# A linear attention with a gated feed-forward on one core: the gates of four chunks by seven block products in place of eight, with the order of the work searched anew

## The chip, the cores and the metric

The kernel runs on one core of one Trainium2 chip. The core has a matrix engine (TensorE, PE in the profile, with its weight loads shown apart as PEld), a vector engine (VectorE, DVE), a scalar engine (ScalarE, ACT), a general engine (GpSimd, POOL) and SyncE (SP), which here only starts transfers. Each engine works through its own queue of instructions in the order in which they stand there; waits between engines go by semaphores. Sums of matrix products are made in eight banks of PSUM, each 128 partitions of 512 f32 numbers. Data and results lie in HBM and are moved to and from the on-chip memory SBUF by DMA.

The metric is the time of one execution on the device in microseconds (us), of which a lower one is better.

## The reference

Inputs are q, k and v of 8 batches, 8 heads, 576 rows and 64 columns, and four weight matrices: w1 and w2 (512 x 1024), w3 (1024 x 1024) and w_out (1024 x 512).

```python
def phi(x):
    return np.where(x > 0, x, np.exp(x) - 1.0) + 1.0
q_p, k_p = (phi(q), phi(k))
kv = np.einsum('bhsd,bhse->bhde', k_p, v)
z = np.sum(k_p, axis=2)
num = np.einsum('bhsd,bhde->bhse', q_p, kv)
den = np.einsum('bhsd,bhd->bhs', q_p, z)[..., None] + 1e-06
x = (num / den)  # heads side by side: 4608 tokens x 512
a = x @ w1
b = x @ w2
h = a * b @ w3
out = h @ w_out
```

## The kernel before

Tokens are in 36 tiles of 128 (two sets of 64 rows of one batch each); four tiles make a chunk of 512 tokens, of which there are nine, 0 to 8. All matmuls are bf16, all sums f32.

The weights come first: w3 and w_out are multiplied into one matrix wf = w3 @ w_out (steps T3, FW), which is kept in bf16, so that the feed-forward is two products by w1 and w2 (the gates a and b), their elementwise product, and one product by wf.

The whole program is a list of steps, the string `ORDER`. A step is written `KIND.arguments`, with a last letter for the engine where there is a choice (`a` ACT, `v` DVE, `p` POOL, `s` SP). The steps are emitted in the order of the string, so the string sets the order of each engine's queue; nothing moves them later. The steps that matter:

- `LQ`, `LK`, `LV` (b, h): load of q, k or v of batch b and half h of the heads, 576 KB each, on SP's queue.
- `PT`, `EX`, `PM` (q or k, b, h): phi, as max(x,0)+1 on DVE, exp(x) on ACT and the minimum of both on DVE.
- `VC` (b, h): cast of v to bf16. `KB` (b): the products of k by v on PE, then a copy.
- `QD` (b, h): transpose of phi(q) by DMA on SP's queue. `ND` (t): numerator and denominator of tile t. `NT` (t): those of the three tiles t to t+2, a "trio", 48 small matmuls into two tiles of PSUM, then 1/denominator (tile `r`) on DVE; `NM` (t, i): the four multiplies with r on DVE that make the tokens `xn` of the trio.
- `XD` (c, m): transpose of two token tiles of chunk c to `xt` by DMA on SP's queue.
- `F` (c, f): for chunk c and block f of 128 gate columns: four matmuls 128x512 for a, four for b, a copy of a to SBUF on ACT, and a multiply with b on DVE, which makes `ab`.
- `O` (t): eight matmuls of the `ab` of tile t by wf, and a copy to `o_sb` by ACT or DVE. `S` (t): its store, two pieces of 128 KB, on SP's queue. `Q` (35): the last tile in narrower pieces with its own stores.

PSUM is split: four banks named "mm", which a, b and the O tiles take, and two tiles "at" of two banks each, which the trios and the attention take. A tile of a bank is free again when what reads it is done. Buffers of SBUF rotate: four for the exp, four for each phi, five for `o_sb`, thirteen of 128x1152 f32 for raw loads ("ld").

In the profile the a and b matmuls are line 483, the ACT copy of a 492, the DVE multiply 494, the O matmuls 536 and their copies 543, the numerators 399, r 431 to 433, their multiplies 405, the phi of PT 286 and PM 294, the cast of v 328, exp 274, and the loads 158.

Of the kernel before, what the change touches and what calls it, by code (L numbers as in the profile page):

```python
# [58 lines left out]
S.26.s S.27.s F.7.7 F.8.0 F.8.1 F.8.2 O.28.v O.29.v S.28.s O.30.a O.31.v F.8.3 S.29.s S.30.s S.31.s
F.8.4 F.8.5 F.8.6 F.8.7 O.32.v O.33.v S.32.s O.34.a S.33.s S.34.b Q.35  # L60
"""


@with_exitstack
def kernel(
    ctx: ExitStack,
    tc: tile.TileContext,
    q: bass.AP,
    k: bass.AP,
    v: bass.AP,  # L70
    moe_w1: bass.AP,
# [532 lines left out]
```

## Time and profile before

| What | Value |
| --- | --- |
| Median of the device time, 3 runs | 241.37 us (241.37 to 241.63) |
| Profiled execution: span, and the median of the runs less the span | 239.7 us, 1.7 us |
| Instructions in it | 5540 |
| PE busy | 233.2 us, 97% of the span |
| DVE busy | 151.0 us, 63% |
| ACT busy | 115.0 us, 48% |
| POOL busy | 8.1 us, 3% |
| Read from HBM, written to it | 38.80 MB, 9.44 MB |

Busy time is the union of the times in which an engine had an instruction at work. The span runs from the first to the last instruction of the profiled execution; the profile has no other time of that execution, and the median of the runs is 1.7 us longer than its span. Groups are shown as line, engine, operation, output<-inputs with partitions x elements and type, the count after an x, then busy us and mean ns of one, then the engine's idle time ahead of them and what ended most of it. The mean of one matmul (380 ns for 128x512) holds its pipelined end, so that four of them in a row take less than four times as long.

### The profile page before, as it was taken

The page shows a single profiled execution, that of the slowest core. Times are in us where ns is not written, and L with a number is a line of the kernel's source. Part 1 is how long each engine was busy: PE and PEld are TensorE (multiplying, and loading weights), DVE is VectorE, ACT ScalarE, POOL GpSimd, SP SyncE. Part 2 cuts the span into 40 slices and gives each one's busy share as a digit, 9 for nine tenths or more (in the row PEclk, how much of TensorE's full clock was granted, in tenths as well). Part 3 has the DMA queues.
Part 4 walks back from the last instruction along what each step waited for, and adds up shares of the span by engine and source line. Part 5 has one row for each costly group of instructions (what it writes and reads, how often), then busy time and mean ns, then how long its engine had stood idle before and what let it go on. Part 6 is the DMA issues. An engine that isn't in the chain of part 4 may idle for free.

```text
span 239.7 us, 5540 instructions
## 1 busy us (share of the span) xinstructions
PE 233.2 (97%) x2276; PEld 120.2 (50%) x2276; DVE 151.0 (63%) x278; ACT 115.0 (48%) x173; POOL 8.1 (3%) x15
## 2 busy tenths in 40 slices
PE   8899999999999999999999999999999999999994
PEld 5656668555445444444454444545444444444443
DVE  0347787889999646877862588885546363433341
ACT  2576743979793255568522656424232113321300
POOL 1020053000000000000000000000000000000000
PEclk9999999999999999999999999999999999999999
DMA  6999999999996999999879959965293763005216
GB/s 241 402 406 397 379 375 390 390 390 389 396 332 137 158 357 247 323 406 296 190 106 192 392 123 262 320 116 131 52 178 69 174 157 88 3 0 125 50 24 154
DMA packets 52553, 55.81 MB, mean 233 GB/s; under 512 B 31280, under 2 KB 32560, under 8 KB 52528
## 3 DMA queue, kind: packets, MB, share of 16 engines
q1 hardware_dynamic: 52288, 55.19, 78.5%
q8 instruction: 18, 0.29, 0.5%
q10 hardware_dynamic: 240, 0.26, 0.3%
q14 instruction: 7, 0.06, 0.1%
HBM read 38.80 MB, written 9.44 MB: 201 GB/s over the span
## 4 chain that ended last, share of the span: by engine, by line
PE 96%; DVE 1%; ACT 1%; issue 0%
PE o_ps L536 26%; PE a_ps L483 25%; PE b_ps L483 24%; PE wf_ps L264 6%; PE nd L399 3%; PE w3p L252 3%; PE warm L149 2%; PE kbp L341 2%; PE a_ps L516 2%; PE b_ps L516 2%; PE xp L458 1%; PE qp L369 1%; PE kvp L341 1%; ACT wo_sb L218 0%; ACT w3b L238 0%; DVE w3t L253 0%
## 5 line engine op out<-in xcount | busy, mean ns | idle before, releaser
L483 PEld LDWEIGHTS <-w_sb 128*128 128x128 bf16 x544 | 52.6, 98 | 62.5 <-DVE xt L459 0.3
L494 DVE TENSOR_TENSOR ab<-a_sb,b_ps 128x512 bf16<-128x512 f32 x68 | 46.2, 686 | 39.9 <-PE b_ps L483 38.6
L492 ACT COPY a_sb<-a_ps 128x512 f32<-128x512 f32 x68 | 39.8, 586 | 64.0 <-PE a_ps L483 63.6
L483 PE MATMUL a_ps<-xt,w_sb 128*128 128x512 bf16 x272 | 69.9, 380 | 0.0
L483 PE MATMUL b_ps<-xt,w_sb 128*128 128x512 bf16 x272 | 69.8, 379 | 0.0
L536 PE MATMUL o_ps<-wf_sb,ab 128*128 128x512 bf16 (+2 forms) x304 | 65.2, 368 | 0.0
L536 PEld LDWEIGHTS <-ab 128*128 128x128 bf16 x304 | 28.4, 98 | 31.7 <-issue 0.4
L543 ACT COPY o_sb<-o_ps 128x512 f32<-128x512 f32 x22 | 12.9, 586 | 33.5 <-PE o_ps L536 26.7
L405 DVE TENSOR_TENSOR xn<-nd,r 128x512 bf16<-128x512 f32 (+2 forms) x47 | 23.8, 559 | 0.3
L274 ACT ACTIVATE ek<-k 128x1152 bf16<-128x1152 f32 x16 | 18.7, 1172 | 0.7 <-ACT ek L274 0.7
L274 ACT ACTIVATE eq<-q 128x1152 bf16<-128x1152 f32 x16 | 18.7, 1168 | 0.4 <-DMA q<-in_q_dram 0.4
L543 DVE COPY o_sb<-o_ps 128x512 f32<-128x512 f32 x13 | 9.0, 691 | 15.3 <-PE o_ps L536 12.6
L264 PE MATMUL wf_ps<-wo_sb,w3t 128*128 128x512 bf16 x64 | 15.6, 380 | 0.5 <-ACT wo_sb L218 0.5
L286 DVE TENSOR_SCALAR phq<-q 128x1152 bf16<-128x1152 f32 x16 | 12.0, 755 | 2.7 <-DMA q<-in_q_dram 2.7
L294 DVE TENSOR_TENSOR phk<-phk,ek 128x1152 bf16<-128x1152 bf16 x16 | 11.9, 750 | 1.8 <-ACT ek L274 1.7
L294 DVE TENSOR_TENSOR phq<-phq,eq 128x1152 bf16<-128x1152 bf16 x16 | 12.1, 755 | 1.0 <-ACT eq L274 0.8
L286 DVE TENSOR_SCALAR phk<-k 128x1152 bf16<-128x1152 f32 x16 | 12.0, 753 | 0.0
L264 PEld LDWEIGHTS <-w3t 128*128 128x128 bf16 x64 | 5.9, 98 | 5.8 <-issue 0.7
L328 ACT CAST vt<-v 128x1152 bf16<-128x1152 f32 x7 | 8.1, 1162 | 0.9 <-DMA v<-in_v_dram 0.9
L253 ACT CAST w3t<-w3p 128x512 bf16<-128x512 f32 x7 | 4.0, 587 | 9.3 <-PE w3p L252 7.4
L399 PEld LDWEIGHTS <-qt 64*64 64x64 bf16 x576 | 6.1, 106 | 4.3 <-issue 4.1
L399 PE MATMUL nd<-kv,qt 64*64 64x65 bf16 x576 | 7.6, 194 | 0.4 <-DVE w3t L253 0.4
(57 smaller groups left out, 127.4 us busy)
## 6 DMA issues: line engine op xcount, KB each, us to landing
q<-in_q_dram SPq DMA_DIRECT2D x16, 576.0 KB, 8.3
k<-in_k_dram SPq DMA_DIRECT2D x16, 576.0 KB, 9.5
v<-in_v_dram SPq DMA_DIRECT2D x16, 576.0 KB, 10.5
out_dram<-o_sb SPq DMA_DIRECT2D x69, 128.0 KB, 2.5
w<-in_moe_w_dram SPq DMA_DIRECT2D x7, 512.0 KB, 10.9
wo<-in_moe_w_out_dram SPq DMA_DIRECT2D x4, 512.0 KB, 8.2
wa<-in_moe_w_dram SPq DMA_DIRECT2D x4, 512.0 KB, 10.7
wb<-in_moe_w_dram SPq DMA_DIRECT2D x4, 512.0 KB, 10.4
```

What stands on the lines that cost most here:

```text
L264: nc.tensor.matmul(wfs[i], w3ts[i][:, c, :], wo_sb[:, c, :], start=(c == 0), stop=(c == FC - 1))
L274: nc.scalar.activation(out=t, in_=raw[n, b, h], func=AF.Exp)
L286: (nc.gpsimd if e == "p" else nc.vector).tensor_scalar(out=by_set(n, t), in0=by_set("k", raw[n, b, h]), scalar1=0.0, scalar2=1.0, op0=ALU. ...
L294: nc.vector.tensor_tensor(out=t, in0=t, in1=by_set("k", es[n, b, h]), op=ALU.min)
L399: nc.tensor.matmul(dst[g * R:(g + 1) * R], qts[b, a // 2][rows, j, a % 2 * R:(a % 2 + 1) * R], kvs[b][rows, a // 2, a % 2, :], start=True, ...
L405: nc.vector.tensor_tensor(out=xn[:, :, a0:a1], in0=n4[:, :, :, 0:D], in1=r.unsqueeze(3).to_broadcast([P, 2, a1 - a0, D]), op=ALU.mult)
L483: nc.tensor.matmul(ops_[key][:, tiles.start * P:tiles.stop * P], w[:, w_row(kc), f * P:(f + 1) * P], xts[c0][:, tiles, kc, :], start=(kc = ...
L492: nc.scalar.copy(out=a_sbs[c0, f], in_=ops_[key])
L494: nc.vector.tensor_mul(out=abs_[c0][:, f, :], in0=a_sbs[c0, f], in1=ops_[key])
L516: nc.tensor.matmul(p, w[:, w_row(kc), f * P:(f + 1) * P], xts[c0][:, 2 * g:2 * g + 2, kc, :], start=(kc == 0), stop=(kc == KC - 1))
L536: nc.tensor.matmul(o_ps, abs_[c0][:, f, m * P:(m + 1) * P], wf_sb[:, f, cols], start=(f == 0), stop=(f == FC - 1))
L543: copy_of(e)(out=o_sbs[t], in_=o_ps)
```

## The change

For the pairs of chunks (5, 6) and (7, 8) the 32 steps F are replaced by the Strassen form in Winograd's version. A pair's gate for one side (a by w1 or b by w2) is a product of matrices that are each cut in 2 x 2 blocks: over the 512 inputs (two halves of 256) and the gate columns (two halves of 512) for w, and over the inputs and the two chunks for x. The four output blocks are then sums of seven products of blocks and not of eight. New steps:

- `WP` (c, f, side, i): product i of 1 to 7 for pair c, block f (0 to 3) and side 0 or 1: two matmuls 128x512 into a bank. The products 1, 5 and 6 are copied to SBUF by ACT; 2, 3 and 7 are added from the bank to such a copy by DVE; product 4 of side 0 is copied by ACT and of side 1 multiplied from the bank on DVE. For side 1, the results of 2, 3 and 7 are then multiplied with those of side 0 by POOL (f32 by f32 to bf16, 24 of them).
- `WS` (side, i): the sums of blocks of the weights, and `WT` (c, i): those of the blocks of xt, on DVE, 128x1024 bf16 each, eight of each.
- `RB`: the "at" tiles' pool is closed and their four banks are opened as single ones ("bk"), which the products take.

Eight output tiles stand in place of five: three of every eight take the space of `w3t`. `ORDER` is the same up to the step `PT.k.2.0`, about 60 us into the span, and another one behind it: all attention now stands ahead of the first WP. Of the changed string the diff shows the place of the bank change only.

```diff
+PAIRS = (5, 7)
+WIDE = ()
...
 ORDER = """
...
+NM.27.2 NT.33 S.8.s NM.33.0
+WS.1.4.v S.9.s O.12.a WS.0.4.v O.18.a XD.7.0 NM.33.1 NM.33.2 NT.30 WT.5.1.v WT.5.2.v NM.30.0 NM.30.1
+NM.30.2 XD.8.1 RB WP.5.1.0.1 WP.5.0.0.1 O.17.v WP.5.0.0.5 WP.5.1.0.5 WT.5.3.v WP.5.0.0.6 XD.8.0
...
+WP.7.3.1.4 O.31.v S.21.s O.29.v S.29.s S.31.s O.20.v O.33.v S.23.s O.34.a S.20.s S.33.s O.32.v S.34.b
+O.28.v S.32.s O.30.a S.28.s S.30.s Q.35
...
+    def ws_of(side, i):
+        if side == 0:
+            return wo_sb.rearrange("p c n -> p (c n)").rearrange("p (i r n) -> p i r n", i=4, r=2)[:, i - 1]
...
+    def s_WS(side, i, e):
+        w = (w1_sb, w2_sb)[side]
+        a, b, op = {1: (w_half(w, 0, 1), w_half(w, 1, 1), ALU.add),
+                    2: (ws_of(side, 1), w_half(w, 0, 0), ALU.subtract),
+                    3: (w_half(w, 0, 0), w_half(w, 0, 1), ALU.subtract),
+                    4: (w_half(w, 1, 0), ws_of(side, 2), ALU.subtract)}[i]
+        (nc.gpsimd if e == "p" else nc.vector).tensor_tensor(out=ws_of(side, i), in0=a, in1=b, op=op)
+
+    def s_WT(c0, i, e):
+        b11, b12, b21, b22 = x_half(c0, 0), x_half(c0 + 1, 0), x_half(c0, 1), x_half(c0 + 1, 1)
+        a, b = {1: (b12, b11), 2: (b22, xs_of(c0, 1)), 3: (b22, b12), 4: (b21, xs_of(c0, 2))}[i]
+        (nc.gpsimd if e == "p" else nc.vector).tensor_tensor(out=xs_of(c0, i), in0=a, in1=b, op=ALU.subtract)
+
+    def w_mm(ps, c0, f, side, i, first):
...
+        for r in range(2):
+            nc.tensor.matmul(ps, lhs[:, r, f * P:(f + 1) * P], rhs[:, :, r, :],
+                             start=(first and r == 0), stop=(r == 1), skip_group_check=not first)
...
+    def w_add(c0, f, side, ps, tmp, c, g, e):
+        nc.vector.tensor_tensor(out=tmp, in0=ps, in1=tmp, op=ALU.add)
+        if side == 0:
+            wtmp[c0, f, "a", c, g] = tmp
+        else:
+            (nc.gpsimd if e == "p" else nc.vector).tensor_mul(
+                out=w_ab(c0, f, c, g), in0=wtmp.pop((c0, f, "a", c, g)), in1=tmp)
+
+    def s_RB(e):
+        at_pool.close()
+        pools["bk"] = at_pool.enter_context(tc.tile_pool(name="bk", bufs=1, space=bass.MemoryType.PSUM))
+
+    def s_WP(c0, f, side, i, e):
+        q = c0, f, side
+        bank = q + ("z" if i in (3, 5) else "x" if i == 2 else "y",)
+        if i == 2:
+            wbank[bank] = mm_tile("wx" + "ab"[side], bank)
+        elif i in (1, 5):
+            wbank[bank] = take("bk", bank, [P, NCH], F32, "w" + bank[3] + "ab"[side])
+        ps = wbank[bank]
+        w_mm(ps, c0, f, side, i, i in (1, 2, 5))
+        if i in (1, 5, 6):
+            t = wtmp[q + (i,)] = w_tmp({1: "e", 5: "phq", 6: "phk"}[i], "p" + str(i) + "ab"[side])
+            nc.scalar.copy(out=t, in_=ps)
+        elif i == 2:
+            w_add(c0, f, side, ps, wtmp.pop(q + (1,)), 0, 0, e)
+            give("mm", bank)
+        elif i == 3:
+            w_add(c0, f, side, ps, wtmp.pop(q + (6,)), 1, 0, e)
+            give("bk", bank)
+        elif i == 7:
+            w_add(c0, f, side, ps, wtmp.pop(q + (5,)), 1, 1, e)
+        elif side == 0:
+            t = wtmp[c0, f, "a", 0, 1] = w_tmp("a_sb", "p4a")
+            nc.scalar.copy(out=t, in_=ps)
+        else:
+            nc.vector.tensor_mul(out=w_ab(c0, f, 0, 1), in0=wtmp.pop((c0, f, "a", 0, 1)), in1=ps)
+        if i == 4:
+            give("bk", bank)
...
```

How the instructions stand. The first place is DVE behind the last step that both orders share, `PT.k.2.0` (the first row; `vt_74` or `vt_78` is the v of an even or odd batch, `phk` and `phq` the phi of k and q). Before:

```order
L286 TENSOR_SCALAR phk<-k 128x1152
L294 TENSOR_TENSOR phk<-phk,ek 128x1152
L294 TENSOR_TENSOR phq<-phq,eq 128x2x9x64
L328 CAST vt_74<-v 128x18x64
L494 TENSOR_TENSOR ab<-a_sb,b_ps 128x512 x2
L286 TENSOR_SCALAR phk<-k 128x1152
```

With the change:

```order
L301 TENSOR_SCALAR phk<-k 128x1152
L343 CAST vt_78<-v 128x18x64
L309 TENSOR_TENSOR phq<-phq,eq 128x2x9x64 x2
L509 TENSOR_TENSOR ab<-a_sb,b_ps 128x512
L301 TENSOR_SCALAR phq<-q 128x2x9x64
L509 TENSOR_TENSOR ab<-a_sb,b_ps 128x512
```

The cast `VC.3.1` of v of batch 3 now stands directly behind the phi of k, and the first gate's multiply (F.1.1) behind that cast and two multiplies of phi of q.

On SP, at the same place, the loads before, beginning with `LV.3.0`, `LV.2.1` and `LV.3.1`:

```order
L158 DMA v<-in_v_dram 128x2x576 x3
L158 DMA q<-in_q_dram 128x2x576
L549 DMA out_dram<-o_sb 64x512 x2
L158 DMA q<-in_q_dram 128x2x576
L158 DMA v<-in_v_dram 128x2x576
```

With the change:

```order
L173 DMA v<-in_v_dram 128x2x576 x3
L173 DMA k<-in_k_dram 128x2x576
L173 DMA q<-in_q_dram 128x2x576
L173 DMA k<-in_k_dram 128x2x576 x2
L173 DMA q<-in_q_dram 128x2x576
```

A load of k of batch 5 now stands ahead of q of batch 2, and the stores of the first output tiles have moved back.

The second place is the bank change. On PE before, the end of the last trio, there NT.33, followed by an O:

```order
L399 LDWEIGHTS qt
L399 MATMUL nd<-kv,qt 64x65
L536 LDWEIGHTS ab
L536 MATMUL o_ps<-wf_sb,ab 128x512
L536 LDWEIGHTS ab
```

With the change, the end of the last trio, now NT.30 (`wya` is a bank of a product for side a):

```order
L414 LDWEIGHTS qt
L414 MATMUL nd<-kv,qt 64x65
L645 LDWEIGHTS w_sb
L645 MATMUL wya<-xt,w_sb 128x512
L645 LDWEIGHTS w_sb
```

The products `WP.5.1.0.1` and `WP.5.0.0.1` follow the trio directly, and an O (O.17) only behind them. On DVE, with the change, from the first multiply of the trio NT.33 on (`ws` and `wo_sb` are sums of weights, `xs` sums of xt):

```order
L420 TENSOR_TENSOR xn<-nd,r 128x512
L629 TENSOR_TENSOR ws<-w_sb,ws 128x1024
L629 TENSOR_TENSOR wo_sb<-w_sb,wo_sb 128x1024
L420 TENSOR_TENSOR xn<-nd,r 128x2x192
L420 TENSOR_TENSOR xn<-nd,r 128x2x64
L420 TENSOR_TENSOR xn<-nd,r 128x512
L446 TENSOR_SCALAR r<-nd 128x14
L447 TENSOR_SCALAR r<-nd 128x10
L448 RECIPROCAL r<-r 128x24
L634 TENSOR_TENSOR xs<-xt 128x1024
L634 TENSOR_TENSOR xs<-xt,xs 128x1024
L420 TENSOR_TENSOR xn<-nd,r 128x512
```

Two sums of weights stand between the multiplies of NT.33, and two sums of xt between r and the multiplies of NT.30.

More of the change, by code (lines that the diff above doesn't have):

```diff
@@ L93 @@
     ps = ctx.enter_context(tc.tile_pool(name="ps", bufs=1, space=bass.MemoryType.PSUM))
-    free = {"ld": deque(range(13)), "mm": deque(range(4)), "at": deque(range(2))}
+    at_pool = ctx.enter_context(ExitStack())
+    pools = {"mm": ps, "at": at_pool.enter_context(tc.tile_pool(name="at", bufs=1, space=bass.MemoryType.PSUM))}
+    free = {"ld": deque(range(13)), "mm": deque(range(4)), "at": deque(range(2)), "bk": deque(range(4))}
     turns = {"w3t": 3, "e": 4, "phk": 4, "phq": 4, "kv": 2, "qt": 4, "xn": 3, "xt": 4, "r": 4,
@@ L530, in s_FP, with ab_of @@
             f_out(c0, f, side)
+    def ab_of(c0, f):
+        for c in range(2):
+            if c0 - c in PAIRS and c0 - c not in WIDE:
+                return quads[c0 - c, f % 4][:, c, f // 4]
+        return abs_[c0][:, f]
     def o_mm(t, cols):
@@ L535, in o_mm @@
         for f in range(FC):
-            nc.tensor.matmul(o_ps, abs_[c0][:, f, m * P:(m + 1) * P], wf_sb[:, f, cols],
+            nc.tensor.matmul(o_ps, ab_of(c0, f)[:, m * P:(m + 1) * P], wf_sb[:, f, cols],
                              start=(f == 0), stop=(f == FC - 1))
@@ L541, in s_O @@
         o_ps = o_mm(t, slice(0, DM))
-        o_sbs[t] = take("o_sb", None, [P, DM], F32, "o_sb")
+        if t % 8 in (1, 4, 6):
+            o_sbs[t] = take("w3t", None, [P, FC, P], BF16, "o_sb").rearrange("p c t -> p (c t)").bitcast(F32)
+        else:
+            o_sbs[t] = take("o_sb", None, [P, DM], F32, "o_sb")
         copy_of(e)(out=o_sbs[t], in_=o_ps)
         give("mm", "o_ps")
+        c0 = t // CT - (t // CT - 1 in PAIRS)
+        if c0 in PAIRS and c0 not in WIDE:
+            n = uses["o", c0] = uses.get(("o", c0), 0) + 1
+            if n == 2 * CT:
+                for f in range(FC // 2):
+                    give("ld", ("abq", c0, f))
     def store(queues, t, o_sb, cols):
@@ L563, in s_Q, with late, w_half, x_half @@
             store((nc.sync, nc.scalar), t, o_sb, slice(pieces[0][0], pieces[-1][1]))
+    quads, wsum, xsum, wbank, wtmp, uses = {}, {}, {}, {}, {}, {}
+    def late(key, n):
+        t = take("ld", key, [P, HW], F32, key[0]).bitcast(BF16)[:, 0:n * NCH]
+        return t
+    def w_half(w, k, fh):
+        return w[:, 2 * k:2 * k + 2, fh * NCH:(fh + 1) * NCH]
+    def x_half(c0, k):
+        return xts[c0][:, :, k::2, :]
+    def ws_of(side, i):
+        if side == 0:
+            return wo_sb.rearrange("p c n -> p (c n)").rearrange("p (i r n) -> p i r n", i=4, r=2)[:, i - 1]
+        key = ("ws", side, (i - 1) // 2)
+        if key not in wsum:
+            wsum[key] = late(key, 4).rearrange("p (i r n) -> p i r n", i=2, r=2)
+        return wsum[key][:, (i - 1) % 2]
@@ new lines, in xs_of @@
+    def xs_of(c0, i):
+        key = ("xs", c0, (i - 1) // 2)
+        if key not in xsum:
+            xsum[key] = late(key, 4).rearrange("p (i m r n) -> p i m r n", i=2, m=CT, r=2)
+        return xsum[key][:, (i - 1) % 2]
+    def s_WS(side, i, e):
[5 more added lines that the diff above has]
+        (nc.gpsimd if e == "p" else nc.vector).tensor_tensor(out=ws_of(side, i), in0=a, in1=b, op=op)
@@ new lines, in w_tmp, with w_ab @@
+    def w_tmp(kind, name):
+        if kind == "a_sb":
+            return take(kind, None, [P, NCH], F32, name)
+        t = take(kind, None, [P, HW], BF16, name)
+        return t.bitcast(F32)[:, 0:NCH]
+    def w_ab(c0, f, c, g):
+        if c0 in WIDE:
+            if c0 + c not in abs_:
+                abs_[c0 + c] = take("ab", None, [P, FC, NCH], BF16, "ab")
+            return abs_[c0 + c][:, f + 4 * g]
+        if (c0, f) not in quads:
+            quads[c0, f] = late(("abq", c0, f), 4).rearrange("p (c g n) -> p c g n", c=2, g=2)
+        return quads[c0, f][:, c, g]
```

101 lines of the change are left out of this document (62 added, 39 removed).

## The prediction

> **What bounds the kernel now.** I read the first part of the page for the busiest engine, its chain that ended last for what the end hangs on, then the groups for durations and the stretches for how full each engine is.
>
> ```profile
> span 239.7 us, 5540 instructions
> PE 233.2 (97%) x2276; PEld 120.2 (50%) x2276; DVE 151.0 (63%) x278; ACT 115.0 (48%) x173; POOL 8.1 (3%) x15
> PE 96%; DVE 1%; ACT 1%; issue 0%
> 59.77:236.14 176.37, 176.37 (x1665) 83.66 (x1664) 111.07 (x201) 76.48 (x117) 0.00 (x0) 1.00 0.73 186
> 213.66 6.91 PE o_ps L536 x32
> 229.20 6.96 PE o_ps L536 x48
> ```
>
> PE is 96% of the chain. The fourth row is the stretch 59.77:236.14 (PE, PEld, DVE, ACT, POOL busy, granted clock, DMA share, GB/s): PE is never idle there, at clock 1.00. The fifth row, of the chain in order of time, prices a 128x512 matmul: 6.91 / 32 = 0.216 us. The last row ends at 236.16; what follows, 239.7 − 236.16 = 3.5 us, is copy and stores. So the end moves with PE: a matmul removed is worth 0.216 us, and a PE wait added costs its whole length. The profiled execution's span is 239.7, the median 241.37; the 1.7 us outside the span I add unchanged.
>
> **The part removed.** A pair's gates took 16 F, each 4+4 matmuls, for two chunks: 256 matmuls for both pairs. They become 112 products of 2: 224. The 32 that go are worth 32 x 0.216 = −6.9 us. Were that all, the time would be 241.4 − 6.9 = 234.5. The rest of the sum is what the new order adds on a PE that has no slack.
>
> **The part added 1: the bank change.** The last trio, NT.30, fills both "at" tiles. The first products need these banks, and the order puts them right behind NT.30 on PE, O.17 only behind two of them. The first product's wait is on the last multiply that reads the trio's second tile, and DVE has r, two sums of xt (128x1024) and four multiplies to run in between. Such a trio before, here NT.4, had an O behind it, which needs none of this:
>
> ```profile
> 52.76 0.63 PE L399 MATMUL nd<-kv,qt 64*64 64x65 bf16 x48
> 53.33 1.90 PE L536 MATMUL o_ps<-wf_sb,ab 128*128 128x512 bf16 x8
> ...
> 53.29 0.17 DVE L431 TENSOR_SCALAR r<-nd 128x14 f32<-128x14 f32 x1
> 53.48 0.17 DVE L432 TENSOR_SCALAR r<-nd 128x10 f32<-128x10 f32 x1
> 53.69 0.30 DVE L433 RECIPROCAL r<-r 128x24 f32<-128x24 f32 x1
> 54.02 1.95 DVE L405 TENSOR_TENSOR xn<-nd,r 128x512 bf16<-128x512 f32 x4
> 55.89 0.75 DVE L286 TENSOR_SCALAR phq<-q 128x1152 bf16<-128x1152 f32 x1
> ```
>
> r takes 54.02 − 53.29 = 0.73, the multiplies 55.89 − 54.02 = 1.87. No row has a sum of two bf16 tiles 128x1024; the nearest is phk by ek, both bf16, 128x1152, quoted below, 0.68 from start to start (61.12 to 61.80): 0.68 x 1024 / 1152 = 0.60 each. With 0.15 for the handoff: 0.73 + 1.20 + 1.87 + 0.15 = 3.95, on PE from the end of NT.30, taken as **+4.0**. Bounds: a sum at half that row, 3.4; at the price of two 512-column reads of a bank (1.37, row L494 below), 5.5.
>
> **The part added 2: the trio ahead.** NT.30 itself waits for both "at" tiles from NT.33. DVE has r 0.73, multiplies 1.87, and now two sums of weights between them (1.20, priced as above), with a handoff 3.95; PE's cover is O.12 and O.18, 16 x 0.216 = 3.46. **+0.5**; bounds 0 to 2.0, by the same two prices of a sum.
>
> **The part moved: 60 to 75 us.** The two orders part at 60 us. A step of v's cast now stands on DVE directly behind the phi of k, ahead of the first gate's multiply, and its load lands late:
>
> ```profile
> 50.71 1.27 SPq L158 DMA_DIRECT2D v<-in_v_dram  x1
> ...
> v<-in_v_dram SPq DMA_DIRECT2D x1, 576.0 KB, 12.1
> 60.26 0.76 DVE L286 TENSOR_SCALAR phk<-k 128x1152 bf16<-128x1152 f32 x1
> 61.12 0.76 DVE L294 TENSOR_TENSOR phk<-phk,ek 128x1152 bf16<-128x1152 bf16 x1
> 61.80 0.75 DVE L294 TENSOR_TENSOR phq<-phq,eq 128x1152 bf16<-128x1152 bf16 x1
> 62.46 0.76 DVE L328 CAST vt<-v 128x1152 bf16<-128x1152 f32 x1
> 63.13 1.28 DVE L494 TENSOR_TENSOR ab<-a_sb,b_ps 128x512 bf16<-128x512 f32 x2
> ...
> 59.77 1.03 PE L483 MATMUL a_ps<-xt,w_sb 128*128 128x512 bf16 x4
> 60.63 1.03 PE L483 MATMUL b_ps<-xt,w_sb 128*128 128x512 bf16 x4
> 61.49 1.03 PE L483 MATMUL a_ps<-xt,w_sb 128*128 128x512 bf16 x4
> 62.36 1.03 PE L483 MATMUL b_ps<-xt,w_sb 128*128 128x512 bf16 x4
> 63.22 1.03 PE L483 MATMUL a_ps<-xt,w_sb 128*128 128x512 bf16 x4
> 64.08 1.03 PE L483 MATMUL b_ps<-xt,w_sb 128*128 128x512 bf16 x4
> ```
>
> Issued at 50.71, this v lands at 50.71 + 12.1 = 62.8; its issue lies ahead of the place where the orders part, so the time holds. DVE did two multiplies and another cast from 61.12 to 63.13; now it stands from about 60.9 to 62.8, then does the cast and two multiplies (0.67 each) and F.1.1's multiply at 62.8 + 2.0 = 64.8 to 65.45. That multiply frees the bank that F.1.0's b matmuls take, the sixth group of four, which PE could begin at 64.08 as the last row has it. They begin at 65.5: +1.4. The second wait there is a load. A k of batch 5 is put ahead of q of batch 2 on SP, whose phi and exp (DVE and ACT) stand ahead of F.1.3's multiply and F.1.0's copy:
>
> ```profile
> 54.00:62.00 8.00, 8.00 (x65) 4.13 (x64) 7.80 (x16) 7.20 (x10) 0.00 (x0) 1.00 1.05 389
> 62.56 0.59 ACT L492 COPY a_sb<-a_ps 128x512 f32<-128x512 f32 x1 [1.12 <-PE a_ps L483]
> ```
>
> At 389 GB/s with the DMA full, a 576 KB load takes 590 / 389 = 1.5 us, so that q lands not 1.5 but 3.0 us behind the v, near 65.8. ACT then does its exp and one of k before F.1.0's copy, which I place 0.8 us behind the PE that wants its bank. Together **+2.2**. Bounds: 0, if the loads land some 2 us earlier than in this row; 3.2, if the wait for q reaches PE whole (1.4 + 1.8).
>
> **Are the engines beside PE full later?** Until the first product DVE gets nearly all its phi work of batches 5 to 7 and the weight sums.
>
> ```profile
> 60.26:149.00 88.74, 88.74 (x927) 41.92 (x926) 65.53 (x119) 51.19 (x76) 0.00 (x0) 1.00 0.96 260
> L483 PE MATMUL a_ps<-xt,w_sb 128*128 128x512 bf16 x272 | 69.9, 380 | 0.0
> L494 DVE TENSOR_TENSOR ab<-a_sb,b_ps 128x512 bf16<-128x512 f32 x68 | 46.2, 686 | 39.9 <-PE b_ps L483 38.6
> L492 ACT COPY a_sb<-a_ps 128x512 f32<-128x512 f32 x68 | 39.8, 586 | 64.0 <-PE a_ps L483 63.6
> ```
>
> Before, DVE is 65.5 of 88.7 us busy there. Counting its new steps up to the first product (44 phi, 32 gate multiplies, 36 of numerators, 10 sums, casts and r) by these start-to-start prices gives about 85 of some 89 us. That leaves 4 us of slack, cover enough for the work but not for stalls; gone, each phi more would cost PE 0.67. In the products, 56 operations of 0.686 and four more sums, 41 us, and 56 copies of 0.586, 33 us, stand beside 224 x 0.216 = 48 us of products and 18 O tiles of 1.7, so no engine is full. What can cost is the order: before, a bank was read out 62.56 + 0.59 − 62.36 = 0.8 us after its successor group began; now each of the 112 products is read by a copy or an add, and PE takes the same bank again only some products later. Going through these waits one by one with the prices above, PE is late by 0.1 to 0.2 us at some six of them: **+1.0** (0.3 to 3).
>
> **POOL** gets 24 multiplies of two f32 tiles. The nearest rows:
>
> ```profile
> L222 POOL CAST w_sb<-wa 128x1024 bf16<-128x1024 f32 x3 | 3.3, 1085 | 18.9 <-DMA wa<-in_moe_w_dram 18.9
> L218 POOL CAST wo_sb<-wo 128x1024 bf16<-128x1024 f32 x1 | 1.4, 1368 | 10.1 <-DMA wo<-in_moe_w_out_dram 10.1
> ```
>
> A 512-column multiply reads as many elements as the 1024-column cast: 0.55 (half a cast) to 1.37, taken 1.1. Twenty-four take 26 of 80 us, under cover of the products; only the last five, behind which the last O stand, could show, from 1.3 each on. [...]
>
> **The end.** Q's own matmuls, copies and stores stay. Ahead of Q's stores, SP had S.33 whole and one half of S.34, whose other half went by ACT; now it has S.28 and S.30 whole:
>
> ```profile
> out_dram<-o_sb SPq DMA_DIRECT2D x69, 128.0 KB, 2.5
> ```
>
> One half more is 131 KB at 389 GB/s: **+0.3** (0 to 0.7, both of S.30).
>
> **Sum:** −6.9 + 4.0 + 0.5 + 2.2 + 1.0 + 0.3 = +1.1: span 240.8, time **242.5**. All low ends: −6.9 + 3.4 + 0.3 = −3.2 (238.2); all high ends, −6.9 + 5.5 + 2.0 + 3.2 + 3.0 + 0.7 = +7.5, would need five mishaps.
>
> **The rivals.**
>
> *A, only the bank change costs.* If the loads land so that the cast does not wait, and the waits of the products are hidden, what is left is −6.9 + 4.0 + 0.5 + 0.3 = −2.1: **239.3**, faster. For it: the deciding load's landing is one sample, and 4 us of DVE slack can take a late cast in. Against it: PE waits for F.1.1's multiply within 4 us, before slack can help. It decides if the v lands before 61.4.
>
> *B, the whole gain.* If PE had work during the bank change too: **235**. Against it: nothing stands between NT.30 and the first product.
>
> *C, the clock drops in the gap.* After its last matmul at 236.16 PE idles in the trace of before:
>
> ```profile
> 239.00:239.30 0.30, 0.00 (x0) 0.00 (x0) 0.00 (x0) 0.00 (x0) 0.00 (x0) 0.89 0.00 0
> 239.30:239.60 0.30, 0.00 (x0) 0.00 (x0) 0.00 (x0) 0.00 (x0) 0.00 (x0) 0.50 0.00 0
> ```
>
> The granted clock (third number from the right) falls to 0.50 at about 239.24, 3.1 us after the last matmul. The gap of 4.0 us is longer. If the clock takes as long to come back, 3.1 us at half speed lose 1.6: 242.5 + 1.6 = **244.1**. Against it: one drop does not say that each gap of 3.1 us makes one. [...]
>
> *D, POOL is slow.* At 1.6 us a multiply, the last five end 5 x 0.3 = 1.5 behind the O that read their outputs, and the O of the pair before wait for the sixth and seventh from the end: **244.5** or more. It decides above 1.3 us.
>
> **How the numbers follow.** The forecast 0.50, A 0.30, B 0.05, C 0.10, D 0.05. Its own range is 241.0 to 244.2 (one of its terms gone, or one at its high end). A measurement of this kernel tells 0.2% from no change, 240.9 to 241.9 counts as the same. Of the forecast's 0.50, 0.40 lies above that, 0.07 in it, 0.03 below; of A, 0.27 below and 0.03 in it. Slower: 0.40 + 0.10 + 0.05 = 0.55; same: 0.07 + 0.03 = 0.10; faster: 0.03 + 0.27 + 0.05 = 0.35. Leaving out B, D and the outer ends of A and C, some 0.15, the range is 238.0 to 245.0.
>
> **What would show it.** PE idle about 4 us behind the last trio, its releaser the DVE multiplies, and there the granted clock (C if it falls); DVE idle until about 62.8 behind a phi, released by v's load, and PE idle near 64 to 68; the groups of the products with 224 matmuls; the POOL multiply's mean (D above 1.3 us). It is wrong if PE's gap at the bank change is under 3 us, if PE has no idle time before 75 us, or if the products' stretch has over 3 us of it.

## The result

The changed kernel takes 245.29 us (245.02 to 245.51, 4 runs) against 241.37 us before: a ratio of 1.0157, 95% interval 1.0129 to 1.0185. It is slower by 3.9 us, where the prediction had 242.5 us and a range of 238.0 to 245.0: the sign is right, the size three and a half times too small. The page after:

```profile
span 243.3 us, 5583 instructions
PE 228.9 (94%) x2244; PEld 117.6 (48%) x2244; DVE 176.3 (72%) x318; ACT 126.4 (52%) x197; POOL 38.3 (16%) x39
PE 78%; DMA 8%; DVE 6%; ACT 2%; issue 2%; SPq 2%; ACTq 0%; DVEq 0%
```

PE has 32 matmuls less (2276 to 2244), and yet the span is 3.6 us longer. The third row is the chain's share by engine: 96% PE before, now 78%. The rest of the chain runs over loads and transposes, DVE, ACT and SP, because at some places PE waited for them; a share of the chain is not PE's idle time. Where PE waits stands in its order of time: start, duration, the run of matmuls, and in brackets the idle time ahead with its releaser.

```profile
63.08 1.03 PE L498 MATMUL a_ps<-xt,w_sb 128*128 128x512 bf16 x4
65.30 1.02 PE L498 MATMUL b_ps<-xt,w_sb 128*128 128x512 bf16 x4 [1.19 <-DVE ab L509]
...
68.81 1.02 PE L498 MATMUL a_ps<-xt,w_sb 128*128 128x512 bf16 x4 [0.77 <-ACT a_sb L507]
...
86.35 1.02 PE L498 MATMUL a_ps<-xt,w_sb 128*128 128x512 bf16 x4 [0.65 <-DMA xt<-xn]
...
89.90 0.58 PE L414 MATMUL nd<-kv,qt 64*64 64x65 bf16 x48
90.41 1.04 PE L498 MATMUL a_ps<-xt,w_sb 128*128 128x512 bf16 x4
...
132.72 1.02 PE L498 MATMUL a_ps<-xt,w_sb 128*128 128x512 bf16 x4 [0.84 <-ACT a_sb L507]
...
152.95 0.74 PE L414 MATMUL nd<-kv,qt 64*64 64x65 bf16 x48
157.45 1.89 PE L645 MATMUL wya<-xt,w_sb 128*128 128x512 bf16 x4 [3.75 <-DVE xn L420]
159.12 2.76 PE L557 MATMUL o_ps<-wf_sb,ab 128*128 128x512 bf16 x8
161.72 1.03 PE L645 MATMUL wza<-xs,wo_sb 128*128 128x512 bf16 x4
...
181.25 0.59 PE L645 MATMUL wyb<-xs,w_sb 128*128 128x512 bf16 x2 [0.32 <-DVE p5b L665]
...
223.64 15.74 PE L557 MATMUL o_ps<-wf_sb,abq 128*128 128x512 bf16 x88
```

The bracket starts at a matmul's modelled end, 0.16 us behind the moment at which the next could have started: 4 matmuls from 63.08 would let the next begin at 63.08 + 4 x 0.216 = 63.95, it begins at 65.30, so 1.35 us are lost where the bracket says 1.19. Behind the small matmuls of a trio it is less, 0.07: the trio from 89.90 ends at 90.48, and the gate's matmul behind it, which waits for nothing, starts at 90.41. The waits at 86, 132 and 157 us stand behind a trio. With 0.16 or 0.07 added, the losses are 1.35, 0.93, 0.72, 0.91, 3.82 and 0.48 us.

One loss has no bracket. The 12 matmuls from 157.45 to 161.72 take 4.27 us, at 0.216 they would take 2.59: 1.68 us more. The stretches there (the last three columns are granted clock, DMA share, GB/s):

```profile
157.40:157.60 0.20, 0.15 (x1) 0.13 (x2) 0.00 (x0) 0.00 (x0) 0.00 (x0) 0.63 1.25 267
...
160.60:160.80 0.20, 0.20 (x2) 0.00 (x0) 0.00 (x0) 0.00 (x0) 0.00 (x0) 0.50 1.02 297
160.80:161.00 0.20, 0.20 (x2) 0.12 (x1) 0.00 (x0) 0.00 (x0) 0.00 (x0) 0.84 0.85 184
```

The granted clock falls to one half within the first row and comes back in the last. A mean of 0.63 over 0.20 us is 1.00 for a quarter of it and 0.50 for the rest, so it falls at 157.45; in the same way it comes back at 160.86.

The sum: −6.9 (matmuls) + 2.28 (the two losses at 64 and 68 us) + 0.72 + 0.91 (at 86 and 132 us) + 0.16 (the last trio takes 0.74 where others take 0.58) + 3.82 (the gap at the bank change) + 1.68 (half clock) + 0.48 (products) + 0.36 (the end) = +3.5 us, within 0.1 of the difference of the spans. The end is the span less the last matmul: 243.3 − (223.64 + 15.74) = 3.92 now, 239.7 − 236.16 = 3.56 before. The other 0.3 of the 3.9 us lie outside the span: the profiled execution took 245.32 us, 2.0 more than its span, where it was 1.7 before. What they are, the profile does not show.

### The profile page after: what moved, and what is told of

Same layout as the page of the kernel before. It is cut to its first block, busy times and chain, and to the rows that moved or that the text cites. A ratio compares the mean times of both kernels' runs of the same rounds, so it can differ in the third digit from the quotient of the medians.

```text
span 243.3 us, 5583 instructions
## 1 busy us (share of the span) xinstructions
PE 228.9 (94%) x2244; PEld 117.6 (48%) x2244; DVE 176.3 (72%) x318; ACT 126.4 (52%) x197; POOL 38.3 (16%) x39
## 4 chain that ended last, share of the span: by engine, by line
PE 78%; DMA 8%; DVE 6%; ACT 2%; issue 2%; SPq 2%; ACTq 0%; DVEq 0%
PE o_ps L557 20%; PE a_ps L498 12%; PE b_ps L498 11%; PE wf_ps L279 6%; PE wya L645 5%; PE wyb L645 5%; DMA k<-in_k_dram 5%; PE wzb L645 2%; PE wza L645 2%; PE w3p L267 2%; PE warm L164 2%; DVE xn L420 2%; DMA xt<-xn 2%; SPq L579 2%; PE a_ps L531 2%
## 5 line engine op out<-in xcount | busy, mean ns | idle before, releaser
L498 PEld LDWEIGHTS <-w_sb 128*128 128x128 bf16 x288 | 27.7, 98 | 36.0 <-issue 4.0
L498 PE MATMUL a_ps<-xt,w_sb 128*128 128x512 bf16 x144 | 37.0, 379 | 2.3 <-ACT a_sb L507 1.6
L498 PE MATMUL b_ps<-xt,w_sb 128*128 128x512 bf16 x144 | 37.0, 379 | 1.2 <-DVE ab L509 1.2
L557 PE MATMUL o_ps<-wf_sb,ab 128*128 128x512 bf16 x160 | 37.9, 386 | 0.0
L669 POOL TENSOR_TENSOR abq<-p1a,p1b 128x512 bf16<-128x512 f32 x8 | 10.9, 1370 | 149.2 <-DVE p1b L665 149.2
L509 DVE TENSOR_TENSOR ab<-a_sb,b_ps 128x512 bf16<-128x512 f32 x36 | 24.2, 684 | 9.1 <-ACT a_sb L507 5.1
L507 ACT COPY a_sb<-a_ps 128x512 f32<-128x512 f32 x36 | 20.8, 586 | 17.1 <-PE a_ps L498 15.7
L557 PE MATMUL o_ps<-wf_sb,abq 128*128 128x512 bf16 (+2 forms) x144 | 28.8, 355 | 0.0
L557 PEld LDWEIGHTS <-ab 128*128 128x128 bf16 x160 | 15.3, 100 | 17.7 <-issue 1.7
L557 PEld LDWEIGHTS <-abq 128*128 128x128 bf16 x144 | 13.5, 98 | 14.5
L645 PEld LDWEIGHTS <-w_sb 128*128 128x128 bf16 x96 | 9.4, 99 | 15.8 <-DVE xn L420 3.9
```

What stands on the lines that cost most here:

```text
L498: nc.tensor.matmul(ops_[key][:, tiles.start * P:tiles.stop * P], w[:, w_row(kc), f * P:(f + 1) * P], xts[c0][:, tiles, kc, :], start=(kc = ...
L507: nc.scalar.copy(out=a_sbs[c0, f], in_=ops_[key])
L509: nc.vector.tensor_mul(out=abs_[c0][:, f, :], in0=a_sbs[c0, f], in1=ops_[key])
L557: nc.tensor.matmul(o_ps, ab_of(c0, f)[:, m * P:(m + 1) * P], wf_sb[:, f, cols], start=(f == 0), stop=(f == FC - 1))
L645: nc.tensor.matmul(ps, lhs[:, r, f * P:(f + 1) * P], rhs[:, :, r, :], start=(first and r == 0), stop=(r == 1), skip_group_check=not first)
L669: (nc.gpsimd if e == "p" else nc.vector).tensor_mul(out=w_ab(c0, f, c, g), in0=wtmp.pop((c0, f, "a", c, g)), in1=tmp)
```

## The experiments

The times of the kernel before beside these runs were 241.25, 241.02 and 241.42 us; the changed kernel is taken as 245.3 us from its own runs, which were not made beside them. One thing limits what two profiles can tell of each other: the first gate's matmuls start between 58.95 and 60.27 us in these traces, although on PE all kernels are the same up to there. A difference of a microsecond between two single executions can be that.

### The clock: the sums behind the multiplies

Does the clock fall because the gap is long, or are these matmuls slow anyway? The first run shortens the gap.

```diff
-WT.5.1.v WT.5.2.v NM.30.0 NM.30.1 NM.30.2
+NM.30.0 NM.30.1 NM.30.2 WT.5.1.v WT.5.2.v
```

> The changed kernel with the two sums of xt (WT.5.1, WT.5.2) moved behind the four multiplies of the last trio on DVE, nothing else. Theory (clock): PE's gap at the bank change falls from 3.75 us by the two sums, 1.26 us (154.17 to 155.44 + the handoff), to about 2.5 us, below the 3.1 us after which the granted clock fell in the trace of before, so the 12 matmuls behind it no longer run at half speed (1.7 us): -1.26 - 1.7 = -2.9 us, 242.4 us, granted clock 1.00 throughout. Rival (the slow matmuls behind the gap are slow for another reason, such as the weights of w1 being loaded first, or any gap would do): only -1.3 us, 244.0 us, with matmuls of 0.43 us still there.

Measured: 243.65 us, ratio 1.0085 (1.0052 to 1.0118), over ten executions that lie in two groups: three at 241.6 to 242.2 us, each with a mean granted clock of 1.000, and seven at 243.4 to 244.9, each with 0.992 or 0.993, as the changed kernel has it. The profiled one took 241.57 us:

```profile
155.39 1.04 PE L645 MATMUL wya<-xt,w_sb 128*128 128x512 bf16 x4 [2.68 <-DVE xn L420]
156.26 1.89 PE L557 MATMUL o_ps<-wf_sb,ab 128*128 128x512 bf16 x8
```

The gap is 2.68 us, and behind it four matmuls take 156.26 − 155.39 = 0.87 us, full speed. That fits the theory for this execution, but in the other seven the clock fell behind the same gap, so that its length alone does not decide. The same kernel was therefore profiled in another execution.

> The kernel with the two sums behind the trio's multiplies once more, for a profile of another execution. Theory (clock): an execution near 244 us shows a granted clock below 1.00 behind the gap of 2.8 us, one near 242 us shows 1.00. Rival: an execution near 244 us shows 1.00 and waits elsewhere.

This execution took 244.4 us, with a mean clock of 0.992:

```profile
153.16 0.74 PE L414 MATMUL nd<-kv,qt 64*64 64x65 bf16 x48
156.50 1.67 PE L645 MATMUL wya<-xt,w_sb 128*128 128x512 bf16 x4 [2.60 <-DVE xn L420]
...
156.60:156.80 0.20, 0.20 (x2) 0.08 (x2) 0.20 (x1) 0.00 (x0) 0.00 (x0) 0.91 1.13 207
160.00:160.20 0.20, 0.20 (x2) 0.10 (x1) 0.00 (x0) 0.00 (x0) 0.00 (x0) 0.56 0.80 143
```

The same program with the same gap (2.60 us), but the clock falls at 156.76 and comes back at 160.18. So one length of gap loses the clock in one execution and keeps it in another.

### The clock: PE busy with nothing useful

The gap stays in the useful work, but PE is kept busy with matmuls of zeros.

```diff
-NT.30 WT.5.1.v
+NT.30 H.7.0 WT.5.1.v
```

> The changed kernel with seven matmuls of zeros (128x256 f32, 0.46 us each, 3.2 us in all), whose result nobody reads, put on PE between the last trio and the first product; PE has nothing else to do there. They remove no wait: the first product still waits for the last multiply of the trio on DVE. Theory (clock): PE is idle under 1 us, the granted clock stays at 1.00, and the 1.7 us of half speed behind the gap go: 243.6 us. Rival (the clock is not the cause of the 0.43 us matmuls, or the DVE chain is what is slow): no change, 245.3 us.

Measured: 243.42 us, ratio 1.0085 (1.0057 to 1.0113), executions 243.2 to 244.0 us, all of them below the changed kernel's lowest 245.0.

```profile
153.11 3.29 PE L164 MATMUL warm<-zero 128*128 128x256 f32 x14
156.95 1.04 PE L645 MATMUL wya<-xt,w_sb 128*128 128x512 bf16 x4 [0.55 <-DVE xn L420]
157.82 1.89 PE L557 MATMUL o_ps<-wf_sb,ab 128*128 128x512 bf16 x8
```

The seven f32 matmuls show as 14. The product still waits for the same multiply on DVE, and yet 1.9 us (1.7 by the two ratios) are won by work that nobody needs: the four products behind it take 157.82 − 156.95 = 0.87 us where they took 1.67. The clock theory holds, at the price that it named (1.7).

The same filling in the kernel with the late sums:

```diff
-NT.30 NM.30.0
+NT.30 H.5.0 NM.30.0
```

> The kernel with the two sums behind the trio's multiplies (gap of 2.84 us in its profile, clock 1.00 there, but other executions up to 3.3 us longer than the fastest), with five matmuls of zeros (2.2 us) put into the gap. Theory (the long executions of that kernel are those in which the clock fell, also behind a gap of 2.8 us): the time stays at the level of its fastest executions, 241.6 to 242.2 us, and the spread shrinks to under 1 us. Rival (the spread has another cause, such as loads landing at other times): executions of 243.4 to 244.9 us are still there.

Measured: 242.63 us, ratio 1.0065 (1.0042 to 1.0089), executions 241.9 to 243.1. The group at 243.4 to 244.9 is gone, and no execution has a clock below 0.997, so that group was the clock. The level is 0.7 us above the expected one and the spread 1.2 us, not under 1: in its profile, at clock 1.00, the waits at 64, 68, 86 and 133 us add up to 4.1 us, against 3.6 us in the profiled execution of the late sums, and its first gate starts 1.0 us later (60.06 for 59.03). Both differ from one execution to the next.

### The front: which step waits for which load

```diff
-PT.k.2.0 LK.5.0 LQ.2.0 VC.3.1.v PM.q.2.1 PM.q.3.1 F.1.1 LK.3.0 PT.q.2.0 F.1.3 LK.5.1 EX.q.2.0 LQ.3.0 EX.k.3.0 VC.2.0.v
+PT.k.2.0 LQ.2.0 LK.5.0 PM.q.2.1 PM.q.3.1 F.1.1 VC.3.1.v LK.3.0 PT.q.2.0 F.1.3 LK.5.1 EX.q.2.0 LQ.3.0 VC.2.0.v
...
-F.1.0 VC.2.1.a
+F.1.0 EX.k.3.0 VC.2.1.a
```

> The changed kernel with, at 60 us, the cast of v (VC.3.1) behind the first gate's multiply on DVE, the load LQ.2.0 ahead of LK.5.0 on SP, and the exp EX.k.3.0 behind F.1.0's copy on ACT. Theory (a stall of a PE without slack is kept to the end): the two PE waits at 64.1 (1.35 us) and 67.7 (0.93 us) go and the time falls by 2.3 us to 243.0 us. Rival (the order behind has to wait for loads or transposes anyway, so an earlier PE waits longer at 85 and 131 us): the two waits go but those at 85.7 and 131.9 grow by as much, 245.0 us.

Measured: 245.31 us, ratio 1.0161 (1.0123 to 1.0199): nothing is won. Two of the four executions (245.75 and 246.54) have a mean clock of 0.986, as if it had fallen twice; the other two, 244.65 and 244.88 at 0.993, are 0.6 and 0.4 below the changed kernel. The profiled one is the first of these, and 0.4 of that is its front (59.22 for 59.62). PE's waits in this run:

```profile
65.75 1.02 PE L498 MATMUL b_ps<-xt,w_sb 128*128 128x512 bf16 x4 [0.33 <-DVE ab L509]
...
68.35 1.02 PE L498 MATMUL b_ps<-xt,w_sb 128*128 128x512 bf16 x4 [0.72 <-DVE ab L509]
70.15 1.02 PE L498 MATMUL a_ps<-xt,w_sb 128*128 128x512 bf16 x4 [0.77 <-ACT a_sb L507]
```

With 0.16 added to each the three waits are 2.3 us, as much as the two before. The cast gone from its place, the next steps that need a load, the phi of q (F.1.3's multiply behind it) and the exp of k (F.1.5's copy behind it), hold PE up instead. Mending one place is not enough; the next run puts every gate's operation of this stretch ahead of every step that waits for a load.

```diff
-PT.k.2.0 LK.5.0 LQ.2.0 VC.3.1.v PM.q.2.1 PM.q.3.1 F.1.1 LK.3.0 PT.q.2.0 F.1.3 LK.5.1 EX.q.2.0 LQ.3.0 EX.k.3.0 VC.2.0.v PM.q.2.0 PM.k.2.0 LK.4.1 QD.2.1 F.1.0 VC.2.1.a F.1.5 F.1.2
+PT.k.2.0 LQ.2.0 LK.5.0 PM.q.2.1 PM.q.3.1 F.1.1 PM.k.2.0 LK.3.0 F.1.3 VC.2.0.v VC.3.1.v LK.5.1 PT.q.2.0 LQ.3.0 EX.q.2.0 PM.q.2.0 LK.4.1 QD.2.1 F.1.0 VC.2.1.a F.1.5 EX.k.3.0 F.1.2
```

> The changed kernel with only the piece at 60 us mended: the multiplies of F.1.1 and F.1.3 ahead of each cast and phi that waits for a load, LQ.2.0 ahead of LK.5.0, the exp of k behind F.1.5's copy. Theory (a stall there is kept to the end): the waits of 1.35 and 0.93 us go without a new one, 243.0 us. Rival (as in the run that moved only the cast, the wait goes to the next step that needs a load, or comes back at 85 and 131 us): 245.0 us, with the same sum of waits.

Measured: 243.81 us, ratio 1.0119 (1.0094 to 1.0143): 1.5 us won of the 2.3. The waits at 64 and 68 us shrink to one of 0.2, and part of what they gave comes back at 86 us:

```profile
85.94 1.02 PE L498 MATMUL a_ps<-xt,w_sb 128*128 128x512 bf16 x4 [1.57 <-DMA xt<-xn]
```

This wait was 0.65 in the changed kernel. PE's trio ahead of it starts 1.3 us earlier (83.79 for 85.12), the transpose lands only 0.4 earlier (85.9 for 86.3). Neither side had it alone: a stall in the front is kept except for what a DMA behind it would have cost anyway.

### Work in the gap

```diff
-S.9.s O.12.a
+S.9.s S.11.s O.12.a
...
-RB WP.5.1.0.1 WP.5.0.0.1 O.17.v
+O.17.v O.16.a RB WP.5.1.0.1 WP.5.0.0.1
...
-WP.5.1.1.7.p S.11.s
+WP.5.1.1.7.p
...
-WP.5.3.0.3 O.16.a
+WP.5.3.0.3
```

> The changed kernel with O.17 and O.16 (8 matmuls each, 3.46 us) between the last trio and the first products on PE, and the store S.11 earlier so that O.16's output tile is free. Theory: 3.46 of the 3.9 us gap are covered with work that has to be done anyway, and the clock holds: -3.46 - 1.7 = -5.1 us, 240.2 us, faster than before by about 1 us. Rival (moving O.16 only opens a wait among the products, where it filled one): the gap goes but PE idles later by up to 1.7 us, 242 us.

Measured: 241.56 us, ratio 1.0018 (0.9990 to 1.0046), no difference from before that can be told. In the profiled execution (242.13 us) the gap is gone and the clock 1.00, but:

```profile
161.01 1.02 PE L645 MATMUL wya<-xs,wo_sb 128*128 128x512 bf16 x4 [1.92 <-ACT p1a L688]
...
159.39 0.58 ACT L567 COPY o_sb<-o_ps 128x512 f32<-128x512 f32 x1 [3.29 <-DMA out_dram<-o_sb]
```

O.16's copy on ACT waits for its output tile, whose store S.11 stands on SP behind those of four other tiles and lands at 159.3; the first product's copy stands behind it on ACT, and PE waits for that. The rival was right in kind (a wait of 1.92 us among the products), though the cause is the store and not the place from which O.16 was taken.

### All together

Late sums, O.17 and O.16 in the gap with S.11 moved up to 140 us, the second mending of the front, and:

```diff
-XD.5.1 F.4.3
+XD.5.1 S.11.s F.4.3
...
-PT.k.7.1 EX.q.6.0 LK.7.0 PM.q.7.0 PT.q.6.0
+PT.k.7.1 LK.7.0 PM.q.7.0 PT.q.6.0
...
-EX.q.6.1 F.4.2 F.4.1
+F.4.2 EX.q.6.0 F.4.1 EX.q.6.1
```

> The changed kernel with every stall that its trace shows taken at its cause: O.17 and O.16 between the last trio and the first products and the two sums of xt behind the trio's multiplies (with S.11's store early, at 140 us, so that O.16's output tile is free in time); at 60 us the gates' multiplies of F.1.1 and F.1.3 ahead of every cast and phi that waits for a load, and the exp of k behind F.1.5's copy; at 130 us the two exps of q of batch 6 behind the copies of F.4.2 and F.4.1. Theory (32 matmuls less are worth 6.9 us as soon as PE is not left waiting): -3.9 (gap) - 1.7 (clock) - 2.0 (front) - 0.8 (130 us) on the changed kernel's 245.3, 236.9 us, 4.4 us faster than the kernel before. Rival (the loads set the pace; an earlier PE waits for them elsewhere): the gap and the clock alone, 239.7 us, with new waits of 2 us or more for DMA between 65 and 150 us.

Measured: 238.87 us (238.5 to 239.2) against 241.02, ratio 0.9915 (0.9893 to 0.9936): faster than both kernels, by 2.1 us and by 6.4 (against the 245.3 of other runs). It lies between theory and rival. The gap, the clock and the wait at 132 us are gone. Two waits for transposes are left, a new one and the one at 86 us, which is larger than it was:

```profile
75.17 0.58 PE L414 MATMUL nd<-kv,qt 64*64 64x65 bf16 x48 [0.94 <-DMA qt<-phq]
...
85.70 1.02 PE L498 MATMUL a_ps<-xt,w_sb 128*128 128x512 bf16 x4 [1.47 <-DMA xt<-xn]
```

### The transposes

```diff
-PT.k.2.0 LQ.2.0 LK.5.0 PM.q.2.1
+PT.k.2.0 LQ.2.0 PM.q.2.1
...
-VC.3.1.v LK.5.1 PT.q.2.0
+VC.3.1.v PT.q.2.0
...
-QD.2.0 EX.q.3.0
+QD.2.0 LK.5.0 LK.5.1 EX.q.3.0
```

> The kernel with all stalls mended (238.9 us) with the loads LK.5.0 and LK.5.1, which nothing needs before 79 us, put behind the transpose QD.2.0 on SP's queue. In that kernel's trace PE waits 1.10 us at 73.8 for QD.2.0 (lands at 75.1) and 1.63 us at 84.0 for XD.2.1 (lands at 85.7). Theory (transposes share the queue with the loads and land behind all that was issued ahead of them): QD.2.0 lands up to 3.0 us earlier, the wait at 73.8 goes, the one at 84 stays since as many bytes lie ahead of XD.2.1 as before: -1.1 us if kept, 237.8 us; more likely the wait at 84 grows by it and the time is 238.9 us. Rival (the transposes are slow in themselves): both waits as they are, 238.9 us, QD.2.0 landing at 75.

Measured: ten executions from 238.2 to 242.2 us; the seven below 241.5 have a median of 239.83 and a ratio of 0.9925 (0.9890 to 0.9960). The ten divide by the clock: six have a mean of 0.991 to 0.993 and lie at 239.7 to 242.2, four have 0.997 to 1.000 and lie at 238.2 to 240.0. The profiled one is of the four, so where the six lost it is not shown. The wait at 75 us is gone, and PE no longer waits for that transpose. In exchange the wait for xt grows and a third transpose is late:

```profile
86.22 1.02 PE L498 MATMUL a_ps<-xt,w_sb 128*128 128x512 bf16 x4 [2.09 <-DMA xt<-xn]
...
145.89 0.51 PE L414 MATMUL nd<-kv,qt 64*64 64x65 bf16 x40 [0.84 <-DMA qt<-phq]
```

That is the likelier outcome named in the expectation. For QD.2.0 the theory holds: it takes 8.5 us from issue to landing with the two loads ahead of it, and 4.1 in the trace of the next kernel, where they stand behind it as here. That PE's trio still starts no earlier (75.22 for 75.17) is the front of this execution, which is 1.05 us later (60.13 for 59.08). Then the load LQ.4.1 behind XD.2.0 and XD.2.1:

```diff
-F.1.7 PT.k.3.1 LQ.4.1
+F.1.7 PT.k.3.1
...
-EX.q.4.0 XD.2.1
+EX.q.4.0 XD.2.1 LQ.4.1
```

> The kernel before this one in the list, with the load LQ.4.1 moved behind the transposes XD.2.0 and XD.2.1 as well. Theory (bytes ahead in the queue decide when a transpose lands): XD.2.1 lands up to 1.5 us earlier and PE's wait at 84 us falls from 1.6 to about 0.2 us, if DVE, whose phi of q of batch 4 stands ahead of a gate's multiply, does not wait for the later load: 236.5 to 237.5 us. Rival (the later load only moves the wait to that phi and the multiply behind it): 238.5 us or more.

Measured: 239.23 us, ratio 0.9910 (0.9879 to 0.9941); the rival's time.

```profile
84.73 1.04 PE L498 MATMUL a_ps<-xt,w_sb 128*128 128x512 bf16 x4 [1.42 <-DMA xt<-xn]
...
60.95 7.50 SPq L401 DMA_TRANSPOSE qt<-phq  x2
...
70.85 8.20 SPq L401 DMA_TRANSPOSE qt<-phq  x2
79.14 2.61 SPq L478 DMA_TRANSPOSE xt<-xn  x2
```

XD.2.1 lands 1.5 us earlier (84.7 for 86.2), but 1.2 of that is the front (58.96 for 60.13), and PE, which is earlier too, still waits 1.42 us. From issue to landing XD.2.1 takes 4.4, 4.1 and 4.2 us in the three last traces: here the load ahead of it made no difference, and the theory does not hold for this transpose. What is late is its issue, at 80.5, the last of the six in the three lower rows: SP issues transposes for 18.3 of the 20.8 us from 60.95 to 81.75. Nor is the rival's mechanism seen, since the wait is not behind the phi. The three last kernels cannot be told apart by their times.

## Why the prediction was wrong

Point by point, by the terms of its sum, in us:

| Step | Predicted | Measured |
| --- | --- | --- |
| 32 matmuls less | −6.9 | −6.9 (2276 to 2244 matmuls, the products at 0.216 each) |
| Gap at the bank change | +4.0 | +3.82 |
| The trio ahead | +0.5 | +0.16 |
| 64 us, the multiply behind the cast | +1.4 | +1.35 |
| 68 us, F.1.0's copy | +0.8 | +0.93 |
| 86 us, xt's transpose; 132 us, the exps of q | none | +0.72, +0.91 |
| Products | +1.0 | +0.48 |
| Half clock behind the gap | rival C, 0.10 | +1.68 |
| End | +0.3 | +0.36 |
| Outside the span | 1.7, unchanged | 2.0 |

**The places it named.** The gap at the bank change is as long as r, two sums and four multiplies on DVE take; of these, the sums and multiplies:

```profile
154.17 0.63 DVE L634 TENSOR_TENSOR xs<-xt 128x1024 bf16<-128x1024 bf16 x1
154.84 0.69 DVE L634 TENSOR_TENSOR xs<-xt,xs 128x1024 bf16<-128x1024 bf16 x1
155.44 1.94 DVE L420 TENSOR_TENSOR xn<-nd,r 128x512 bf16<-128x512 f32 x4
...
62.55 0.76 DVE L343 CAST vt<-v 128x1152 bf16<-128x1152 f32 x1 [1.67 <-DMA v<-in_v_dram]
```

The sums take 155.44 − 154.17 = 1.27 for both, where 1.20 was reckoned from the phi's row. Of the 0.15 taken for the handoff, 0.07 shows, from the last multiply's end at 155.44 + 1.94 = 157.38 to the product at 157.45. The last row is the cast at 60 us: v lands at 62.5 where 62.8 was read off the load's issue, because that issue stands ahead of the place where the two orders part.

**What failed, first: the rival with a chance of 0.10.** The step "one drop does not say that each gap of 3.1 us makes one" is true, but it was used to put the chance near nothing and to leave the drop out of the sum. The price of C came out right, 1.6 for 1.68, and in part by luck: it took the 3.1 us from the last matmul to the drop for the time at half speed, and in the runs that delay is anything from 2.9 to 4.9 us, while the time at half speed is 3.41 us in all four that lost the clock. Five profiles have a gap left open. The clock fell in the four that follow and stayed in the late sums' first one (2.68 us).

| Run | Trio's end | Clock falls | Clock back | At half |
| --- | --- | --- | --- | --- |
| the change | 153.69 | 157.45 | 160.86 | 3.41 |
| late sums, second profile | 153.90 | 156.76 | 160.18 | 3.41 |
| cast moved | 152.86 | 157.79 | 161.20 | 3.41 |
| front mended | 153.20 | 156.32 | 159.73 | 3.41 |

The traces hold the clock's changes themselves: in that of the change the records begin at full speed at 7.27, go to half at 157.45, to full at 160.86 and to half at 242.79 behind the last matmul, and these distances, 150.2, 3.41 and 81.9 us, are 44, 1 and 24 times 3.413. In that of before, the one distance, from 7.13 to 239.23, is 232.1 us, 68 times as much. So stretches of this length, counted from one change, can be laid over a whole trace, also over one whose clock stayed; that the clock keeps to them everywhere is the author's reading, and why it does so is not shown. The stretches about the gap, of the change, of the late sums' second profile, of the cast moved (two) and of the late sums' first profile (two):

```profile
154.04:157.45 3.41, 0.00 (x1) 0.01 (x1) 3.31 (x7) 1.39 (x3) 0.00 (x0) 1.00 1.01 179
153.35:156.76 3.41, 0.81 (x50) 0.50 (x39) 3.05 (x9) 1.66 (x3) 0.00 (x0) 1.00 0.89 200
150.96:154.38 3.42, 1.89 (x54) 0.92 (x52) 3.04 (x9) 1.18 (x3) 0.00 (x0) 1.00 0.79 184
154.38:157.79 3.41, 1.17 (x6) 0.58 (x7) 2.18 (x5) 1.01 (x3) 0.00 (x0) 1.00 1.08 195
151.06:154.48 3.42, 1.65 (x53) 0.84 (x51) 2.98 (x9) 1.39 (x3) 0.00 (x0) 1.00 0.83 195
154.48:157.89 3.41, 2.50 (x12) 1.18 (x13) 2.14 (x5) 1.35 (x3) 0.00 (x0) 1.00 1.10 188
```

The clock falls at the end of the first, second and fourth row, with PE busy for 0.00, 0.81 and 1.17 us of the stretch, and not at the end of the others, with 1.89, 1.65 and 2.50. In the late sums' first profile a stretch ended in the middle of the gap, which left both stretches with more of PE's work. So a stretch was not always empty where the clock fell, and the drop can come when PE is at work again, as with the cast moved, where PE starts at 156.62:

```profile
156.50:157.00 0.50, 0.38 (x2) 0.21 (x3) 0.06 (x1) 0.00 (x0) 0.00 (x0) 1.00 1.35 257
...
157.50:158.00 0.50, 0.50 (x3) 0.19 (x2) 0.00 (x0) 0.50 (x2) 0.00 (x0) 0.79 0.51 111
```

Over all whole stretches of the twelve traces, counted from the first record at full speed on, the nine with PE busy for at most 1.17 us (four at the gap, five at the end of the program) are each followed by half speed, and none of the others, which have 1.57 us or more, is. What happens between the two is not shown. A gap of 2.60 us lost the clock in one execution, and one of 2.68 kept it in another. What C's chance should have been is an estimate from these three numbers, 3.41, 1.17 and 1.57 us, if the stretches may end anywhere: 0.8 to 1 for a gap of 3.8 us, and 0.5 to 0.7 for one of 2.7. By their mean clocks all four executions of the change lost it, and seven of ten of the late sums. The drop belonged in the sum.

**What failed, second: stalls that the sum did not have (+1.63).** "Together +2.2" was the whole stage from 60 to 75 us, and for the stages up to the bank change the prediction counted DVE's work against PE's ("about 85 of some 89 us") and left it there. DVE did have that much work (85.4 us busy from 60.12 to 157.45), but PE waited for single late transfers: at 86 us for a transpose of xt, at 132 us for a copy behind two exps of q whose load came late. Of these places it priced which engine is full, not which transfer lands when. The half about DVE was right, the half "not for stalls" named the cost and gave it no number.

**What was too high.** The trio ahead cost 0.16, within its bounds: in its row at 152.95 the 48 small matmuls take 0.74 where others take 0.58. The prediction let all of them wait for both tiles; the first 28 write only the first tile, which the second of the four multiplies frees, and O.12 and O.18 cover that. The products wait 0.48 in one place, half of what was taken, within its bounds.

**Rival D** did not come about although its condition did in part: POOL's multiplies took longer than the 1.1 us that were taken, eight of them 1.37 us and the other sixteen 1.27, about the 1.3 from which D was to decide,

```profile
L669 POOL TENSOR_TENSOR abq<-p1a,p1b 128x512 bf16<-128x512 f32 x8 | 10.9, 1370 | 149.2 <-DVE p1b L665 149.2
```

and PE runs without a bracket from 223.64 to its end.

**Rival A and B** failed by what they were said to need: the load did not land before 61.4, and nothing filled the gap. The run with everything mended shows how much of B was there to be had: 2.1 of its 6.4 us, and its profile has 2.5 us more in waits for two transposes.

In sum: forecast +1.1, measured +3.6 in the span. 1.68 is the clock and 1.63 the two stalls that were not priced; the terms that were too high give back 0.3 (trio), 0.5 (products) and 0.2 (gap), and the 0.2 that are left are small differences in the other terms. The 0.3 outside the span come on top.
